# One S4D-and-PEER kernel: early query-weight pieces through half a PSUM bank, block 0 in halves, a later third inverse, and products split into rounded parts

## The chip, the cores and the metric

The kernel runs on one core of one Trainium2 chip. The time is device microseconds (us) of one execution, given as the median over several runs. Five engines of the core work side by side, each through its own list of instructions in order: PE (matmul), DVE, ACT and POOL (vector, scalar and general work), and SP, which here only issues DMA transfers. An instruction waits until the semaphores that it names have been raised by the instructions that it depends on; everything behind it on the same engine waits with it.

## What is computed

```python
x = A_u                                                   # 2048 tokens x 512
h = x + S4D(layernorm(x))                                 # K[d,l] = 2 Re sum_n C[d,n] exp(A[d,n] dt[d] l)
                                                          # y = irfft(rfft(u, 4096) * rfft(K, 4096))[:2048] + D*u
q = einsum("nd,dhc->nhc", layernorm(h), w_q)              # 32 heads, 2 x 128
i1 = argmax over e of q[..., :128] . k1[e]                # 16 experts each
i2 = argmax over e of q[..., 128:] . k2[e]
e = i1 * 16 + i2                                          # one of 256 experts per token and head
act = gelu(einsum("nd,nhd->nh", layernorm(h), u[e]))      # the softmax over one candidate is 1
out = h + einsum("nh,nhd->nd", act, v[e])
```

## The kernel before, in words

**First half, the convolution.** The 512 channels are taken in four chunks c of 128. The convolution is an FFT-like product written as matmuls in stages. For every chunk there is the spectrum of the input (`u_s1`, s1u, and `u_s2`, s2yu) and the kernel K: for each of 32 indices i (eight in a chunk) POOL makes phases and magnitudes (`pg` L552, `mg` L581 and L584), ACT takes sines (`t` L639 to L642), DVE multiplies the two into tables (`gf` L646 to L650, `mg` L654 and L659, the last one), PE sums the tables into `kps` (L685, 64 matmuls), and the result goes through s1k (L466) and s2yk (L483). The two spectra are multiplied (for c = 3 on DVE L727 and L728, ACT `ki` L734 and POOL `U` L738), and a first inverse stage `ia` (L759) gives T, of which the chunks 0 to 2 are stored in DRAM and the last stays as T3.

**The weights, beside it.** The query weights w_q are folded with the keys in 32 pieces n: `w_piece` loads 512 KB (`wq`), PE multiplies it with the key matrices ka and kb (`wps` L811, 16 records in the trace), ACT copies the result (`wt` L815), PE transposes it (`wpt` L818), ACT copies again (`wh` L822), and after every fourth piece SP stores 256 KB (`w_d` L825). When all are stored, the four quarters come back (`w_q` L897) and ACT and DVE split each into a rounded part and the rest (`w_hi` L900, `w_lo` L901). These rounded parts have the type fp32r, which PE takes at a faster rate than f32.

**Second half, PEER.** Eight blocks b of 256 tokens: `prefetch` loads Tb, cb and xt; `inverse` makes `ib` (L1005, 64 matmuls, 128 records) and adds x into h (L1012); `center` takes the mean (L1045), `hc` (L1051) and its two parts `hhi` (L1055) and `hlo` (L1059), and the square (L1072); `variance` gives `rstd`; `scores` multiplies hhi, hlo with w_hi, w_lo (`sc` L1115, for each half k of a block 24 matmuls of 512 columns) and with u (`xu` L1122, 12 matmuls of 256 columns); DVE finds the maximum (`mx` L1135, `eq`, `kq`, `ix`), and `select` transposes activations and indices (`ta`, `ixt`), broadcasts the indices (`bc`, `idxb`), builds one-hot masks on DVE (`oh` L1239), counts them on PE (`cnt` L1249), multiplies with the activations (`wt` L1257), multiplies with the expert rows v (`o` L1269, f32, 16 records a block), adds h (`ob` L1274) and stores.

**What sets the order.** One list scheduler, the class `Plan`, writes out the order of all engines' instructions beforehand. Every step is declared with an engine, an estimated cost, what it reads and writes, and which PSUM banks it takes and gives back; `BIAS` moves groups of steps (w0 to w7 are the pieces by four, tab0 to tab31 the tables, cen, inv, sc, sel the steps of a block) earlier or later in the list. `RINGS` says how many buffers a tile has. Seven PSUM banks are shared by most first-half steps (`psA`); until the parameters are done they hold parameter tiles. An eighth, `pc`, holds small statistics of the layernorm (mu_s, rs_s, dv_s) and is otherwise empty.

Of the kernel before, what the change touches and what calls it, by code (L numbers as in the profile page):

```python
# [27 lines left out]
def view(t, off, dims):  # L28
# [5 lines left out]
BIAS = dict(cen0=-321, cen1=200, cen2=494, cen3=497, cen4=149, cen5=340, cen6=-266, cen7=239, e1=358, ia0=-109,  # L34
            ia1=-262, ia2=137, ia3=-186, inv0=-5, inv1=276, inv2=455, inv3=28, inv4=-226, inv5=168, inv6=-279,
            inv7=251, k100=-188, k101=-367, k102=-393, k103=146, k110=-120, k111=-78, k112=285, k113=-195, k120=26,
            k121=138, k122=119, k123=500, k130=281, k131=65, k132=456, k133=-340, k20=1, k21=-267, k22=475, k23=455,
            par=1000, par0=-75, par1=482, pre0=-134, pre1=-400, pre2=-53, pre3=-248, pre4=22, pre5=-190, pre6=-358,
            pre7=-385, sc0=192, sc1=396, sc2=28, sc3=-3, sc4=-333, sc5=-351, sc6=208, sc7=-289, sel0=396, sel1=401,
            sel2=383, sel3=-57, sel4=143, sel5=-134, sel6=-243, sel7=-240, st=-225, tab0=-63, tab1=491, tab10=450,  # L40
            tab11=491, tab12=20, tab13=-259, tab14=96, tab15=242, tab16=320, tab17=48, tab18=-197, tab19=481,
            tab2=-105, tab20=-54, tab21=279, tab22=-344, tab23=-208, tab24=39, tab25=479, tab26=-241, tab27=-22,
            tab28=460, tab29=304, tab3=-332, tab30=-23, tab31=472, tab4=481, tab5=-171, tab6=6, tab7=-393, tab8=-37,
            tab9=-382, u100=-133, u101=99, u102=388, u103=473, u110=-377, u111=-173, u112=-171, u113=187, u120=-335,
            u121=439, u122=-81, u123=-23, u130=-213, u131=-7, u132=-347, u133=-341, u20=464, u21=-49, u22=164,
            u23=-320, var0=185, var1=-128, var2=-164, var3=178, var4=-12, var5=-16, var6=174, var7=157, w0=67,
            w1=-205, w2=320, w3=313, w4=-132, w5=344, w6=500, w7=54, wr=299)
# [3 lines left out]
class Plan:  # L51
# [5 lines left out]
    REST, SLOW = 3.0, 3.5  # L57
# [111 lines left out]
def kernel(ctx, tc, xa, xb, xt, lar, aim, cre, cim, ldt, dsk, wq, ka, kb, ue, ve,  # L169
# [39 lines left out]
    mu_s, rs_s, dv_s = pc[:, 0:64], pc[:, 64:128], pc[:, 128:256]  # L209
# [12 lines left out]
    sg, r64, w2, den, w0, dt, r = (psA.tile([P, 512], F32, tag="s", name=f"par{k}") for k in range(7))  # L222
    x_raw = [wk.tile([P, 32, 128], F32, tag="y", name=f"x{i}", bufs=2) for i in range(2)]
# [49 lines left out]
    def loads():  # L273
        def get(*p):
            for dst, src in p:
                nc.sync.dma_start(dst, src)

        for nm, dst, src in (("ld", ld_, ldt.to_broadcast([P, D])), ("lar", lar_, lar), ("aim", aim_, aim), ("cr", cr_, cre),
                             ("ci", ci_, cim)):
            plan.add("SP", 0.65, lambda dst=dst, src=src: get((dst, src)), w=[(nm, 0), (nm, 1)], lag=0.6)  # L280
        for i in range(8):
            plan.add("SP", 1.55, lambda i=i: get((x_raw[i // 4][:, 8 * (i % 4):8 * (i % 4) + 8], xa[:, 8 * i:8 * i + 8, :])),
                     w=[("x", i)], t=[f"x{i // 4}"], lag=0.6)
        plan.add("SP", 1.0, lambda: get((ca_s, ca.rearrange("p (s m) -> p s m", s=2)), (ka_s, ka), (kb_s, kb)),
                 w=["ca"], lag=0.6)
        plan.add("SP", 6.0, lambda: get((c2_s, c2.rearrange("p (k m) -> p k m", k=32))), w=["c2"], lag=0.6)

    def params():
# [76 lines left out]
        e1 = con.tile([P, 16, 256], F32, tag="T", name="e1")[:, 0:11]  # L365
# [57 lines left out]
        plan.add("SP", 0.45, lambda: nc.sync.dma_start(e_d, e1), r=["e1"], w=["e_d"], t=["e1"], lag=6.0)  # L423
# [4 lines left out]
    plan = Plan(dict(psA=7), BIAS)  # L428
# [29 lines left out]
    def stage1(dst, lhs8, kt, nm, r, tiles, key):  # L458
        for n in range(2):
# [11 lines left out]
            k = plan.add("PE", 0.93, mm, r=r, t=tiles, take="psA", n_mm=16)  # L471
            plan.add("ACT", 0.48, ev, w=[key + (kt, n)], t=tiles, give="psA", after=[k])

    def stage2(c, nm, k4, deps, tiles):
# [10 lines left out]
        return job, plan.add("PE", 0.95, mm, r=deps + ["c2"], t=tiles, take="psA", n_mm=8)  # L485


    def u_s1(c, kt):
# [16 lines left out]
        plan.add("SP", 0.45, load, w=[xs_k], t=[xs_k], lag=3.0)  # L505
# [88 lines left out]
    def factors(i, made):  # L594
# [17 lines left out]
        if i == 16:  # L612
            plan.add("SP", 0.45, e_load, r=["e_d"], w=["E1"], t=["E1"], lag=6.0)
# [55 lines left out]
    def kgen(i):  # L669
# [18 lines left out]
        plan.add("PE", 1.0, mm, r=[("tab", i, k, s) for k in range(2) for s in range(2)], w=[("kps", n)],  # L688
# [60 lines left out]
    def k_ia(c):  # L749
        plan.group = f"ia{c}"  # L750
        deps = [("P", c, k4) for k4 in range(8)]
        for n in range(8):
# [21 lines left out]
            k = plan.add("PE", 1.80, mm, r=deps + ["ca"], t=[f"yk{c}", f"yu{c}" if c > 2 else f"yk{c}", f"U{c}", f"T{c}"], take="psA", n_mm=16)  # L774
# [12 lines left out]
        if c < 3:  # L787
            for r in range(2):
                plan.add("SP", 2.0, lambda r=r: store(r), r=[("T", c, n) for n in range(8)],
                         w=[("t_d", c, r)], t=[f"T{c}"], lag=6.0)  # L790
# [3 lines left out]
    def w_piece(n):  # L794
# [4 lines left out]
        for nm, b, m in (("wq", 2, n), ("wt", 2, n), ("wh", 2, hg)):  # L799
            if m >= b:  # L800
                plan.ring(f"{nm}{m}", f"{nm}{m - b}")

        def load():
            d["in"] = tb.tile([P, 4, 2, 128], F32, tag="wq", name=f"wq{n}")
            nc.sync.dma_start(d["in"], wq[:, n])

        def mm():
            ps = bank(j1, f"wps{n}")
# [580 lines left out]
```

## Time and profile before

| quantity | value |
|---|---|
| median of 3 runs | 541.44 us (540.92 to 541.61) |
| the profiled execution, its own time | 543.62 us |
| its span in the trace | 541.8 us |
| mean granted TensorE clock | 0.974 |
| PE busy | 466.3 us of the span |

The trace holds one execution. Its rows give the start, the time busy, the engine and the line, then what is written and what is read, with the sizes. Behind some rows stands, in brackets, how long the engine was idle before and what released it; "issue" there means that no semaphore explains the wait. A row with x8 stands for eight records of the same form, and a matmul of f32 leaves two records. The time "busy" of a matmul contains its way through the array, so the pace is read from one start to the next.

### The profile page before, as it was taken

The numbers are of one execution on the slowest core, as the hardware profiler recorded it, in microseconds if no ns is written. First come the engines' busy times: TensorE is split into PE (matmuls) and PEld (weight loads), VectorE is DVE, ScalarE is ACT, GpSimd is POOL, SyncE is SP. The second block draws the span as 40 slices with busy tenths as digits, with TensorE's granted clock in tenths as the row PEclk, the third lists the DMA queues.
The fourth block names the chain that finished last, engine by engine and source line by source line (L and its number), as shares of the span: only waits on it lengthen the run. The fifth ranks groups of instructions, "written<-read, shape, count | busy, mean of one in ns | idle before, by whom it ended". The sixth has DMA issues, their size and how long they took to land. (4 is left out here: it accounts for less than half of the span.)

```text
span 541.8 us, 16659 instructions
## 1 busy us (share of the span) xinstructions
PE 466.3 (86%) x7154; PEld 397.4 (73%) x7154; DVE 410.2 (76%) x716; ACT 297.3 (55%) x588; POOL 323.0 (60%) x339
## 2 busy tenths in 40 slices
PE   0045898989999999989995975999999999999996
PEld 0024677869999899979995964878777788888765
DVE  5997857779996898699738643368796695788884
ACT  6543888984899579949973612342323333406220
POOL 0698798999989999996817004161642535066030
PEclk9999799999999999999999888999999999999997
DMA  7984586667204120300065558000402511010011
GB/s 250 404 288 137 144 247 183 194 209 270 80 2 158 41 59 3 158 1 3 2 223 179 187 185 235 0 2 1 157 1 82 182 52 40 1 40 1 2 79 40
DMA packets 27361, 61.30 MB, mean 113 GB/s; under 512 B 2932, under 2 KB 14456, under 8 KB 26136
## 3 DMA queue, kind: packets, MB, share of 16 engines
q1 hardware_dynamic: 27136, 60.11, 33.3%
q8 instruction: 56, 0.92, 0.7%
q14 instruction: 17, 0.14, 0.1%
q10 hardware_dynamic: 152, 0.13, 0.1%
HBM read 46.21 MB, written 14.02 MB: 111 GB/s over the span
## 5 line engine op out<-in xcount | busy, mean ns | idle before, releaser
L552 POOL TENSOR_TENSOR pg<-PS 128x1024 int32<-128x1024 int32 x32 | 68.6, 2148 | 5.2 <-ACT t L639 5.1
L581 POOL TENSOR_TENSOR mg<-TS 128x1024 f32<-128x1024 f32 x32 | 62.6, 1956 | 13.8 <-PE kps L685 12.6
L1150 POOL TENSOR_TENSOR ks<-kq 128x512 f32<-128x512 bf16 x16 | 18.9, 1181 | 58.6 <-DVE kq L1144 58.6
L759 PE MATMUL ia<-ca_s,U 128*128 128x128 f32 x256 | 51.4, 284 | 0.7 <-POOL U L738 0.7
L1239 DVE TENSOR_SCALAR oh<-idxb,ec_s 128x2048 bf16<-128x2048 bf16 (+1 forms) x72 | 47.6, 729 | 5.2 <-ACT idxb L1221 5.2
L1115 PE MATMUL sc<-w_hi,hhi 128*128 128x512 f32 x128 | 45.5, 437 | 0.5 <-DVE eq L1139 0.5
L811 PE MATMUL wps<-wq,ka_s 128*32 128x128 f32 x256 | 15.4, 317 | 35.1 <-DMA wq<-wq 33.3
L640 ACT ACTIVATE t<-t,halfpi 128x512 f32<-128x512 f32 x64 | 42.4, 662 | 2.1
L759 PEld LDWEIGHTS ia<-ca_s,U 128*128 128x128 f32 x256 | 40.6, 200 | 1.0 <-POOL U L738 1.0
L639 ACT ACTIVATE t<-pg 128x512 f32<-128x512 int32 x64 | 39.4, 615 | 3.4 <-DVE gf L647 2.9
L1115 PE MATMUL sc<-w_lo,hhi 128*128 128x512 f32 x128 | 40.7, 400 | 0.0
L1115 PE MATMUL sc<-w_hi,hlo 128*128 128x512 f32 x128 | 40.6, 399 | 0.0
L642 ACT ACTIVATE t<-pg 128x512 f32<-128x512 int32 x64 | 39.2, 614 | 0.8 <-DVE U L730 0.3
L759 PE MATMUL ia<-ca_s,yk 128*128 128x128 f32 x192 | 38.2, 281 | 0.0
L466 PE MATMUL s1u<-c_s,xs 128*64 128x128 f32 x512 | 34.3, 279 | 4.1 <-DVE mg L659 1.1
L584 POOL TENSOR_TENSOR mg<-TS 128x512 f32<-128x512 f32 x32 | 37.4, 1169 | 0.0
L1029 POOL TENSOR_TENSOR hs<-h 128x256 f32<-128x256 f32 x7 | 7.3, 1038 | 48.8 <-DVE h L1012 48.8
L483 PE MATMUL s2yu<-yu,c_s 128*128 128x128 f32 x256 | 32.7, 282 | 4.2 <-DVE gf L647 1.7
L685 PE MATMUL kps<-mg 128*32 128x64 f32 x1024 | 34.1, 230 | 1.9 <-issue 1.0
L811 PEld LDWEIGHTS wps<-wq,ka_s 128*32 128x32 f32 x256 | 5.9, 117 | 40.1 <-DVE pa L329 31.4
L483 PEld LDWEIGHTS s2yu<-yu,c_s 128*128 128x128 f32 x256 | 30.0, 192 | 6.3 <-ACT yk L469 1.8
L466 PEld LDWEIGHTS s1u<-c_s,xs 128*64 128x64 f32 x512 | 28.3, 138 | 8.3 <-issue 4.3
(174 smaller groups left out, 1397.0 us busy)
## 6 DMA issues: line engine op xcount, KB each, us to landing
wq<-wq SPq DMA_DIRECT2D x32, 512.0 KB, 4.3
t_d<-T SPq DMA_DIRECT2D x24, 256.0 KB, 3.7
Tb<-t_d SPq DMA_DIRECT2D x8, 768.0 KB, 5.8
x<-xa SPq DMA_DIRECT2D x8, 512.0 KB, 6.2
xs<-xb SPq DMA_DIRECT2D x16, 256.0 KB, 6.2
xt<-xt SPq DMA_DIRECT2D x8, 512.0 KB, 5.7
out<-ob SPq DMA_DIRECT2D x7, 512.0 KB, 2.7
c_s<-c SPq DMA_DIRECT2D x1, 2048.0 KB, 14.3
```

Source lines behind the costliest of these rows:

```text
L466: T.matmul(ps[64 * k:64 * k + 64, g, :], lhs8(4 * n + g), c1_s[:, k], start=True, stop=True)
L483: T.matmul(ps[:, k, :], c2_s[:, kk, :], y[:, :, kk, :], start=True, stop=True)
L552: G.tensor_tensor(view(pg, 0, [[32, 2 * NC], [8, 4], [1, 8]]), view(t["PS"], 1024 + off, [[1, 2 * NC], [128, 4], [0, 8]]), view(t["PS"], 8 ...
L581: G.tensor_tensor(view(mg, 0, [[96, NC], [8, 8], [1, 8]]), view(ts, 512 + 8 * o, [[8, NC], [1, 8], [0, 8]]), view(ts, 8 * o, [[8, NC], [0, ...
L584: G.tensor_tensor(view(mg, 64, [[96, NC], [8, 4], [1, 8]]), view(ts, 1536 + o, [[1, NC], [64, 4], [0, 8]]), view(ts, 1024 + 8 * o, [[8, NC ...
L639: A.activation(p, pg[:, :, k], AF.Abs)
L640: A.activation(p, p, AF.Sin, scale=-SINSCALE, bias=halfpi)
L642: A.activation(p, pg[:, :, k], AF.Sin, scale=SINSCALE)
L685: T.matmul(kps[32 * q:32 * q + 32, 2 * g + h, :], m[:, d, 64:96], m[:, d, 0:64], start=(e == 0), stop=(e == 1))
L759: T.matmul(ps[:, g, :], t[:, 4 * n + g].rearrange("p a b -> p (a b)"), ca_s[:, s, :], start=(s == 0), stop=(s == 1))
L1115: T.matmul(ps[:, 512 * h:512 * h + 512], t[x_][:, q, ts], I[w_][:, q, 512 * h:512 * h + 512], start=(q == 0 and x_ == w_), stop=(q == 3 an ...
L1239: V.tensor_scalar(oh[:, :, 0:ln], t["idxb"][:, :, sl], S["ec"][:, 4 * e + j:4 * e + j + 1], None, op0=ALU.is_equal)
```

## The change

It has five parts, and a sixth that follows from them.

1. **Early pieces.** The first twelve pieces (`NE = 12`) no longer take banks from `psA`. Their `wps` and `wpt` go to two 128-column parts of the bank `pc`, one of each, so one piece is in each part at a time. Pieces 2 and 3 are loaded into free parts of the parameter tile pb, piece 4 into a free part of the tile e1; ka and kb are loaded before x, and c2 behind it with an own group.
2. **Block 0 in halves.** The mean, hc, hhi, hlo and the square of block 0 are made for 128 columns at a time, and the scores of k = 0 read only the first half. Its variance comes from sums on POOL and two matmuls, as in the other blocks, in place of eight f32 matmuls.
3. **ib of block 2.** The inverses of blocks 2 and later stand behind the first quarter of block 0's scores.
4. **o of rounded products.** The product with the activations is made in place; ACT makes `whi`, DVE `wlo`, and `o` is the sum of three fp32r products (v_hi·whi, v_hi·wlo, v_lo·whi): 24 matmuls a block in place of eight f32 ones. v_hi and v_lo are made once; u and v are loaded into the buffers of w_q. whi and wlo have one buffer each.
5. **Costs in the list.** SP's steps get transfer times as costs with a shorter lag, some PE costs rise a little, REST and SLOW change.
6. `BIAS` has new numbers, so the order differs on all engines.

```diff
-    mu_s, rs_s, dv_s = pc[:, 0:64], pc[:, 64:128], pc[:, 128:256]
+    mu_s, rs_s, dv_s, wps_s, wpt_s = pc[:, 0:64], pc[:, 64:128], pc[:, 128:256], pc[:, 256:384], pc[:, 384:512]
...
-    REST, SLOW = 3.0, 3.5
+    REST, SLOW = 2.6, 6.0
...
+    NE = 12
+    plan = Plan(dict(psA=7, psW=1, psV=1), BIAS)
...
+        early = n < NE
+        home = {2: "pb", 3: "pb", 4: "e1"}.get(n, f"wq{n}")
...
+            j1["o"] = wps_s if early else bank(j1, f"wps{n}")[:, 0]
...
+            j2["o"] = wpt_s if early else bank(j2, f"wpt{n}")[:, 0]
+            T.transpose(j2["o"], d["t"], ident)
...
-        plan.add("SP", 0.45, load, w=[f"wq{n}"], t=[f"wq{n}"], lag=4.5)
-        k = plan.add("PE", 0.55, mm, r=[f"wq{n}", "ca"], t=[f"wq{n}", f"wt{n}"], take="psA", n_mm=16)
+        plan.add("SP", 1.7, load, w=[f"wq{n}"], t=[home], lag=2.6)
+        pa_, pt_ = ("psW", "psV") if early else ("psA", "psA")
+        k = plan.add("PE", 0.55, mm, r=[f"wq{n}", "ka"], t=[home, f"wt{n}"], take=pa_, n_mm=16)
...
-                             take="psD" if k is None else None, after=[] if k is None else [k], n_mm=32)
+                             take="psD" if k is None else None, after=[k] if k else [L[0]["sc"]] if b > 1 else [], n_mm=32)
...
+        if b == 0:
+            for a in range(2):
+                sl, job = slice(128 * a, 128 * a + 128), {}
...
+                k = plan.add("PE", 0.95, mm, r=["cst", ("h", b, a)], t=[kh, kc], take="psD", n_mm=8)
...
-                for q in range(4 if first else 1):
-                    lhs = t["hc"][:, q] if first else t["vs"]
-                    T.matmul(ps[:, k:k + 1], lhs[:, 128 * k:128 * k + 128], S["ones"][:, 0:1], start=(q == 0),
-                             stop=(q == 3 or not first))
+                T.matmul(ps[:, k:k + 1], t["vs"][:, 128 * k:128 * k + 128], S["ones"][:, 0:1], start=True, stop=True)
...
+            if q == 0 and k == 0:
+                t["sc"] = last
...
-                            T.matmul(ps[:, q], S["v"][:, e, 128 * (q0 + q):128 * (q0 + q) + 128], t["wt2"][:, e, sl],
-                                     start=(e == 0), stop=(e == 1))
+                            for v_, w_ in (("hi", "hi"), ("hi", "lo"), ("lo", "hi")):
+                                T.matmul(ps[:, q], S["v_" + v_][:, e, 128 * (q0 + q):128 * (q0 + q) + 128],
+                                         t["w" + w_][:, e, sl], start=(e == 0 and v_ == w_), stop=(e == 1 and v_ == "lo"))
```

**The start on PE.** Before, pieces 4 and 5 stand ahead of the first kernel sums (`kps0_0`; the number behind mg and gf is the index i).

```order
L811 MATMUL wps4_449<-wq4_397,ka_s_76 32x128 x4
L811 MATMUL wps4_449<-wq4_397,kb_s_77 32x128 x4
L818 MATMUL wpt4_465<-ident_60,wt4_459 128x128
L811 MATMUL wps5_467<-wq5_419,ka_s_76 32x128 x4
L811 MATMUL wps5_467<-wq5_419,kb_s_77 32x128 x4
L818 MATMUL wpt5_485<-ident_60,wt5_481 128x128
L685 MATMUL kps0_0_491<-mg0_366 32x64 x4
```

Now, with the pieces in `pc`:

```order
L826 MATMUL pc_96<-pb_98,ka_s_76 32x128 x4
L826 MATMUL pc_96<-pb_98,kb_s_77 32x128 x4
L834 MATMUL pc_96<-ident_60,wt2_382 128x128
L690 MATMUL kps0_0_412<-mg0_276 32x64 x4
...
L826 MATMUL pc_96<-wq5_358,kb_s_77 32x128 x4
L834 MATMUL pc_96<-ident_60,wt4_465 128x128
L826 MATMUL pc_96<-wq6_380,ka_s_76 32x128 x4
L826 MATMUL pc_96<-wq6_380,kb_s_77 32x128 x4
L690 MATMUL kps0_0_412<-mg1_352 32x64 x4
```

The sums of i = 0 moved ahead of pieces 4 and 5, and those of i = 1 stand alone behind pieces 4 to 6; each transpose here waits for a copy on ACT, and each second product for the copy of the one before it.

**The end of the convolution on PE.** Before, the last pieces are multiplied ahead of the last s2yk, and two transposes are left behind it:

```order
L811 MATMUL wps31_4129<-wq31_2888,ka_s_76 32x128 x4
L811 MATMUL wps31_4129<-wq31_2888,kb_s_77 32x128 x4
L483 MATMUL s2yk3_0_4140<-yk3_4012,c2_s_85 128x128 x4
...
L483 MATMUL s2yk3_7_4223<-yk3_4012,c2_s_85 128x128 x4
L818 MATMUL wpt30_4230<-ident_60,wt30_4138 128x128
L818 MATMUL wpt31_4234<-ident_60,wt31_4145 128x128
```

Now:

```order
L488 MATMUL s2yk3_4_4087<-yk3_3957,c2_s_85 128x128 x4
L826 MATMUL wps28_4094<-wq28_3923,ka_s_76 32x128 x4
...
L488 MATMUL s2yk3_7_4153<-yk3_3957,c2_s_85 128x128 x4
L826 MATMUL wps30_4164<-wq30_4108,ka_s_76 32x128 x4
L826 MATMUL wps30_4164<-wq30_4108,kb_s_77 32x128 x4
L834 MATMUL wpt30_4178<-ident_60,wt30_4175 128x128
L826 MATMUL wps31_4186<-wq31_4149,ka_s_76 32x128 x4
L826 MATMUL wps31_4186<-wq31_4149,kb_s_77 32x128 x4
L834 MATMUL wpt31_4216<-ident_60,wt31_4195 128x128
L764 MATMUL ia3_0_4221<-ca_s_86,yu3_2813 128x128
```

Pieces 28 to 31 moved into and behind the last s2yk, and the last stage `ia3` stands behind piece 31.

**The way into PEER on PE.** Before, with the mean of block 0 in one and the inverse of block 2 ahead of the first scores:

```order
L1045 MATMUL mean0_4535<-h0_4476,ones_d_4157 128x256 x4
...
L1005 MATMUL ib2_0_4571<-cb2_4515,Tb2_4495 32x64 x3
...
L1115 MATMUL sc0_0_4646<-w_hi_4154,hhi0_4566 128x512 x2
L1115 MATMUL sc0_0_4646<-w_lo_4155,hhi0_4566 128x512 x2
L1115 MATMUL sc0_0_4646<-w_hi_4154,hlo0_4605 128x512 x2
L1084 MATMUL var0_4660<-ones_d_4157,hc0_4559 128x1 x8
```

Now:

```order
L1086 MATMUL mean0_0_4454<-h0_4451,ones_d_4207 128x128 x4
...
L1086 MATMUL mean0_1_4499<-h0_4451,ones_d_4207 128x128 x4
...
L1143 MATMUL sc0_0_4524<-w_hi_4204,hhi0_4497 128x512 x2
...
L1029 MATMUL ib2_0_4588<-cb2_4534,Tb2_4478 32x64 x3
...
L1117 MATMUL var0_4687<-ones_d_4207,vs0_4624 128x1 x2
```

The mean stands in two halves, the first of them directly behind ib of block 0, and ib of block 2 moved behind the first scores.

221 lines of the change are left out of this document (121 added, 100 removed).

## The prediction, made before the changed kernel was run

> **What bounds the kernel now.** I first read the page's busy shares and then a table of windows cut at the borders of the stages (its columns: window, length, busy us of PE, PE's weight loads, DVE, ACT and POOL with counts, the granted TensorE clock, the share of the DMA engines, GB/s).
>
> ```profile
> PE 466.3 (86%) x7154; PEld 397.4 (73%) x7154; DVE 410.2 (76%) x716; ACT 297.3 (55%) x588; POOL 323.0 (60%) x339
> ...
> 31.40:60.00 28.60, 17.39 (x298) 11.76 (x300) 24.75 (x77) 15.21 (x37) 26.22 (x26) 1.00 0.58 175
> 60.00:280.00 220.00, 209.64 (x4102) 189.28 (x4100) 178.89 (x294) 179.00 (x354) 191.88 (x170) 0.98 0.35 113
> 280.00:296.00 16.00, 10.82 (x130) 9.92 (x126) 11.09 (x17) 7.17 (x16) 9.59 (x8) 0.98 0.55 165
> 313.40:340.00 26.60, 17.28 (x425) 14.51 (x425) 10.00 (x14) 5.42 (x7) 6.06 (x6) 0.87 0.63 190
> 340.00:525.00 185.00, 183.55 (x1915) 146.44 (x1914) 141.13 (x201) 62.51 (x102) 74.48 (x100) 1.00 0.13 44
> ```
>
> PE sets the time. It is full from 340 to 525 and close to full from 60 to 280, and idle ahead of the first piece (until 31.4), 28.6 − 17.39 = 11.2 us from there to 60, 5.2 us at the end of the convolution, 9.3 us on the way into PEER, and in the tail. A term of the sum is therefore either PE work that disappears in a full stage, or PE idle time that gets filled or shortened.
>
> **The start (parts 1 and 6).** These rows give the place.
>
> ```profile
> 36.29 0.65 PE L811 MATMUL wps<-wq,ka_s 128*32 128x128 f32 x8 [1.68 <-DMA wq<-wq]
> 36.69 0.68 PE L811 MATMUL wps<-wq,kb_s 128*32 128x128 f32 x8
> 38.64 0.65 PE L811 MATMUL wps<-wq,ka_s 128*32 128x128 f32 x8 [1.27 <-ACT wt L815]
> 40.10 0.47 PE L818 MATMUL wpt<-ident,wt 128*128 128x128 f32 x1 [0.39 <-ACT wt L815]
> 49.01 0.44 PE L685 MATMUL kps<-mg 128*32 128x64 f32 x8 [0.58 <-DVE mg L659]
> 71.13 0.32 PE L685 MATMUL kps<-mg 128*32 128x64 f32 x8
> ...
> POOL mg L581 <- PE kps L685: 11.4, 6, 2.7
> ```
>
> The first kernel sums start at 49.01, when DVE has finished the tables of i = 0 and 1 together. The list now makes table 0 first and lets its sums go ahead of pieces 4 and 5. Pieces no longer take banks that the parameters hold. I put the sums of i = 0 at about 44, 5 us earlier. POOL's magnitudes wait for these sums; six such waits between 60 and 280 add up to 11.4 us (the last row), so part of the 5 us goes on down the chain: nothing at least, 5 at most. I take 3, since the sums of i = 1 now stand behind pieces 4 to 6, whose transposes wait for ACT. The sums of i = 3, at 71.13 before, would then start near 68.
>
> What lies ahead of them differs. By the order, before that point PE had done pieces 0 to 10 and four s1u jobs; now it does pieces 0 to 11 and none of these s1u. In the full stage behind it stood 21 pieces, and now 16, since 28 to 31 moved to the last s2yk.
>
> ```profile
> 70.11 1.09 PE L466 MATMUL s1u<-c_s,xs 128*64 128x128 f32 x16
> 279.41 0.33 PE L818 MATMUL wpt<-ident,wt 128*128 128x128 f32 x1
> 279.67 1.97 PE L466 MATMUL s1k<-c_s,k 128*64 128x128 f32 x32
> 281.57 0.43 PE L811 MATMUL wps<-wq,ka_s 128*32 128x128 f32 x8
> 282.58 7.41 PE L483 MATMUL s2yk<-yk,c_s 128*128 128x128 f32 x64
> ```
>
> Two products take 282.58 − 281.57 = 1.01 us, a transpose 279.67 − 279.41 = 0.26, so a piece costs 0.76. Five fewer give 3.8; four s1u jobs of 1.09 more take 4.4. The term is 3 + 3.8 − 4.4 = **2.4 us**. Bounds: −0.6 if the sums come no earlier, and 8.4 if all 5 us arrive and about 4 of POOL's 11.4 us go too. The waits of the single bank are on PE's list as well: twelve pieces with two trips to ACT each, 24 trips. At the 0.39 of row 40.10 they come to 9.4 us, which the 11.2 idle us of this stretch hide; the third rival is about the case where they don't.
>
> **The end of the convolution (part 6).** PE stands idle here while DVE multiplies the spectra, and ia3 then runs slowly.
>
> ```profile
> 295.22 0.61 PE L759 MATMUL ia<-ca_s,yu 128*128 128x128 f32 x2 [5.02 <-DVE yu L727]
> 296.56 0.80 PE L759 MATMUL ia<-ca_s,U 128*128 128x128 f32 x2 [0.72 <-POOL U L738]
> 302.27 0.40 PE L759 MATMUL ia<-ca_s,yu 128*128 128x128 f32 x2
> 302.50 0.39 PE L759 MATMUL ia<-ca_s,U 128*128 128x128 f32 x2
> ...
> 296.00:300.00 4.00, 3.44 (x16) 3.44 (x17) 0.90 (x4) 0.04 (x1) 0.51 (x1) 0.50 0.97 377
> ```
>
> From 296.56 to 302.27 the granted clock is 0.50 and ia3 goes at about half the pace it has from 302.27 on (0.23 a row). At full pace these 5.7 us would be 2.9. Pieces 28 to 31 now fill part of the gap. From 36 to 48 PE was at 0.40 us a row of eight records, not the 0.22 to 0.24 of 281.57, though it worked almost half of the time; so a partly filled stretch need not raise the clock; here, though, PE comes into the gap at the full pace and only has to keep it. Between 0 and 2.9 I take the middle, **1.4 us**. The Trainium skill ("TensorE: Matmul & The Clock Gate", Part 1: The HAM clock gate) says that the clock goes to half after a whole idle window of about 3.4 us; by that the filled gap would keep it full and this term would be 2.9. The 5.02 idle us with the slow rows behind them agree with it; what a partly filled gap does, no run here shows.
>
> **The way into PEER (parts 2 and 3).** Now the chain from the inverse of block 0 to the first scores.
>
> ```profile
> 316.79 1.29 DVE L1012 TENSOR_TENSOR h<-ib,xt 128x512 f32<-128x512 f32 x2 [0.80 <-PE ib L1005]
> 321.76 2.47 PE L1045 MATMUL mean<-h,ones_d 128*128 128x256 f32 x8
> 324.27 1.22 DVE L1051 TENSOR_TENSOR hc<-h,mean 128x1024 f32<-128x1024 f32 x1 [1.71 <-PE mean L1045]
> 328.00 1.74 DVE L1059 TENSOR_TENSOR hlo<-hc,hhi 128x1024 fp32r<-128x1024 f32 x1
> 333.39 1.22 PE L1115 MATMUL sc<-w_hi,hhi 128*128 128x512 f32 x2
> 336.12 1.98 PE L1084 MATMUL var<-ones_d,hc 128*128 128x1 f32 x16
> ...
> PE ib L1005 <- issue: 8.2, 3, 5.0
> ```
>
> The operands of the scores are ready at 328.00 + 1.74 = 329.7, but PE is still in ib of block 2, where it stood for 5.0 us without a semaphore to wait for; the scores start at 333.39. Now: half of h at 317.4, half a mean (1.24) 318.7, half of hc 0.6, of hhi as much again (an estimate from hc, of the same size), of hlo 0.9, and handing over: about 321.2. PE meanwhile does half of ib1, the other half mean and more of ib1, some 4 us, and if the wait of about 2 us for "issue" that it has at ib1 stays, the scores start at 324.6, 8.8 us earlier. The rest of ib1 and ib2 still has to be done behind them; from 319.60 to 319.71 four records took 0.11 us at a lowered clock, and half of it is the least that a full clock can give, so these 192 records are 2.6 to 5.3 us.
>
> ```profile
> 319.60 0.34 PE L1005 MATMUL ib<-cb,Tb 128*32 128x64 f32 x3
> 319.71 0.34 PE L1005 MATMUL ib<-cb,Tb 128*32 128x64 f32 x3
> ```
>
> I take 3.3, nearer to the full clock, since these records now stand between scores: 8.8 − 3.3 = **5.5 us**. If the 5.0 us for "issue" come back behind the scores, 0.5 remain; without any such wait (2 us more, and 2.6) it is 8. The variance has two matmuls, four records, in place of 16: at 1.98 / 16 each it saves **1.5 us**, and the sums for it lie on POOL, busy 6.06 of 26.6 us here. If POOL were late, rstd would be, and xu's bank with it, not the scores.
>
> **o (part 4).** A whole block's o stands between xu and cnt.
>
> ```profile
> 510.12 0.28 PE L1122 MATMUL xu<-u_hi,hhi 128*128 128x256 f32 x1
> 511.56 3.62 PE L1269 MATMUL o<-wt,v_s 128*128 128x256 f32 x16
> 515.11 1.06 PE L1249 MATMUL cnt<-oh,hs_s 128*32 128x256 bf16 x32
> ```
>
> o takes 515.11 − 511.56 = 3.55 us. The twelve xu ahead of it, fp32r with 256 columns, the form that o gets, take 1.44, 0.12 each. 24 of them are 2.88, so a block saves 0.67, and blocks 0 to 6 save **4.7 us**, on a PE that is 183.55 of 185 us busy. By the Trainium skill ("TensorE: Matmul & The Clock Gate", Part 1) 256 columns take 256 / 2.4 GHz + 2.5 ns = 109 ns, and by that the term would be 6.5; the rows of xu are above it, so I stay with 0.12. The new DVE work (wlo, like the wt below 0.41 for half a block) is 0.7 to 0.8 us a block; DVE works 141.13 of 185 us, and ACT, which makes whi, 62.51, which hides both. Without that cover the eight blocks would cost 6 us.
>
> **The tail.**
>
> ```profile
> 517.80 1.23 DVE L1135 TENSOR_REDUCE mx<-sc 128x64 f32<-128x1024 f32 x1 [0.43 <-PE sc L1115]
> 525.89 6.42 DVE L1239 TENSOR_SCALAR oh<-idxb,ec_s 128x1024 bf16<-128x1024 bf16 x16 [0.21 <-ACT idxb L1221]
> 533.41 0.42 DVE L1257 TENSOR_TENSOR wt<-cnt,actT 128x256 f32<-128x256 f32 x1 [0.77 <-PE cnt L1249]
> 533.38 4.29 PE o L1269 x32
> ```
>
> Behind the last scores the chain is DVE's. Block 7 adds whi, wlo (0.3 + 0.8) and 48 products for o, 2.9 us at half of 0.12 and 5.8 at the pace of 256 columns, against 4.29. Ahead of its masks DVE gets block 6's wlo and its wait for cnt. That is 1 to 4 us longer. On the other side o of block 5 and half an xu, 2.88 + 1.44 us of PE, now stand behind the last scores, which come that much earlier. I set the tail to **0**, from −2 to +2.
>
> **Sum.** 2.4 + 1.4 + 5.5 + 1.5 + 4.7 + 0 = 15.5 us. The profiled execution of 543.62 us (span 541.8, 1.8 around it) would become 528.1. It lies 2.2 above the median of 541.44, so the forecast is 541.44 − 15.5 = **525.9**. All lower bounds together (−0.6, 0, 0.5, 1.5, 4.7, −2) save 4.1, which is 537.3; all upper ones (8.4, 2.9, 8, 1.5, 4.7, 2) save 27.5, which is 513.9.
>
> **Rivals.**
> *The start gives nothing and the gap closes late.* Piece 31 now stands ahead of ia3 on PE, and its load waits on SP behind a store of earlier pieces.
>
> ```profile
> wq<-wq SPq DMA_DIRECT2D x32, 512.0 KB, 4.3
> ```
>
> A load lands 4.3 us after its issue (the row's last number). If ia3 starts 3 us later and the sums no earlier, the first two terms become −0.6 and −3, and the time is 541.4 − 8.1 = 533. For it speaks that the store and the reload of w_q follow that piece too; against it that DVE, not PE, ends the gap by 5.02 us. Chance 0.22.
> *The start gives more.* POOL's 11.4 us of waits come from the same chain, PE stays at the full clock at 295, and no "issue" comes in the way: near 515. Chance 0.14.
> *Slower: the one bank at the start.* All twelve pieces go through it, and a copy on ACT stands in line with the sines. At the 1.27 us of row 38.64, 24 trips are 30.5 us, 19 more than PE has idle there; POOL then waits at every table, and with 13.1 us of other gains the end would be near 548. It decides from (11.2 + 13.1) / 24 = 1.0 us a trip. Most trips before (0.39) are far below. Chance 0.06.
> *The change does not do what it says:* the terms spend themselves in waits that this trace can't show, and the time stays within 0.2%: 0.04.
>
> **Numbers.** The forecast has 0.54, with its own range of 519 to 531. Faster by over 0.2% (about what a measurement of this kernel can tell from none) is 0.54 + 0.22 + 0.14 = 0.90, within it 0.04, slower 0.06. The range from 513 to 536 leaves out the slow rival, no change and a little of both ends.
>
> **What would show it.** Right: the first sums near 44 and those of i = 3 near 68; a start of ia3 no later behind the last s2yk's begin than 14 us (282.58 to 296.56); the first scores 9 us nearer to ib0; o at about 2.9 us a block. Wrong: waits of PE for `wt` or `wh` of 1 us and more in a row in the first 70 us; an ia3 that waits for a piece; an "issue" of 5 us that only moves behind the first scores; DVE above 90% in the blocks.

## The result, and the profile after

The changed kernel takes 546.83 us (median of 10 runs, 542.55 to 551.14); the kernel before, measured beside it, 541.21 (10 runs, 534.49 to 544.0). The ratio is 1.0105, its 95% interval 1.0059 to 1.0151. A second set of 12 runs gave 544.74 against 541.93 and 1.0057 (1.0008 to 1.0105). So the change is slower by 0.6 to 1%; 525.9 and faster had been forecast. (The ratios leave out disturbed runs, so they can differ a little from the quotient of the medians.)

The page of the changed kernel gives the busy time of each engine as before, and its windows are cut at its own stages (columns as in the prediction).

```profile
PE 466.2 (86%) x7222; PEld 398.9 (74%) x7222; DVE 424.7 (79%) x728; ACT 300.5 (56%) x598; POOL 327.6 (61%) x342
```

```profile
28.80:60.00 31.20, 17.97 (x306) 12.20 (x308) 26.33 (x79) 15.82 (x39) 29.59 (x30) 0.90 0.56 191
60.00:280.00 220.00, 205.63 (x4004) 187.00 (x4002) 180.82 (x297) 175.45 (x343) 189.88 (x170) 0.98 0.31 98
280.00:297.30 17.30, 15.36 (x220) 13.43 (x215) 10.59 (x16) 10.23 (x24) 9.11 (x8) 1.00 0.60 199
311.00:340.00 29.00, 23.53 (x467) 19.85 (x466) 18.37 (x26) 9.30 (x15) 7.49 (x9) 0.94 0.80 250
340.00:525.00 185.00, 179.46 (x2069) 142.99 (x2071) 157.15 (x227) 65.52 (x113) 77.56 (x100) 0.99 0.14 50
525.00:540.80 15.80, 11.25 (x68) 10.61 (x57) 2.56 (x5) 0.81 (x2) 0.00 (x0) 0.50 0.13 34
```

PE has as much to do as before (466.2 against 466.3 us). Between 60 and 280 it is busy 4.0 us less than before (205.63 against 209.64 of the same 220 us); between 340 and 525, mostly blocks, it is idle 5.5 of 185 us where it was 1.5; and the last 15.8 us run at a granted clock of 0.50. The chain of waits shows what the end of the tail consists of (start, length, engine, line):

```profile
522.16 2.47 DVE oh L1269 x6
...
524.67 0.84 PE cnt L1279 x29
...
525.96 0.34 DVE wlo L1294
...
526.34 10.30 PE o L1309 x47
...
536.67 0.69 DVE ob L1314
```

The o of block 7 alone takes 10.30 us on the path that sets the end; before it was 4.29.

To see where the time went I cut both executions at four marks: the start of the last s2yk, the first scores, the end of the last scores, and the end. Each kernel was profiled a second time later (last two columns).

| stretch | forecast | before | after | difference | before, again | after, again | difference |
|---|---|---|---|---|---|---|---|
| start to last s2yk | −2.4 | 282.58 | 284.41 | +1.8 | 281.6 | 282.1 | +0.5 |
| to first scores | −10.2 | 50.8 | 39.65 | −11.2 | 47.3 | 39.9 | −7.4 |
| to end of last scores | −7.2 | 184.3 | 183.0 | −1.3 | 187.7 | 182.1 | −5.6 |
| to the end | +4.3 | 24.1 | 33.8 | +9.7 | 24.5 | 33.8 | +9.3 |
| span | −15.5 | 541.8 | 540.8 | −1.0 | 541.1 | 537.9 | −3.2 |

The forecast column is the sum of the prediction, regrouped: 1.4 + 8.8 for the way to the first scores; in the blocks 4.7 + 1.5, less 3.3 for the displaced ib, and 4.3 for the o of block 5 and the half xu that move behind the last scores, which then stand against it in the tail.

The spans are 1.0 and 3.2 us shorter, the medians 5.6 and 2.8 us longer. That is the choice of executions: those of the change were among its shorter ones (4.3 and 5.1 us below the medians), those of the kernel before lay above the medians that these are set against (by 2.4 and 1.0 us). So the traces show where the gain of 15.5 us is missing, but not what makes the other executions of the change longer than the profiled ones. One number is there for every execution, the mean granted clock: its median is 0.972 over 29 runs of the kernel before and 0.963 and 0.964 over the 10 and 12 of the change.

### The profile page after: what moved, and what is told of

The parts are those of the page before. It is cut to its first block, busy times and chain, and to the rows that moved or that the text cites. A ratio compares the mean times of both kernels' runs of the same rounds, so it can differ in the third digit from the quotient of the medians.

```text
span 540.8 us, 16831 instructions
## 1 busy us (share of the span) xinstructions
PE 466.2 (86%) x7222; PEld 398.9 (74%) x7222; DVE 424.7 (79%) x728; ACT 300.5 (56%) x598; POOL 327.6 (61%) x342
## 5 line engine op out<-in xcount | busy, mean ns | idle before, releaser
L1269 DVE TENSOR_SCALAR oh<-idxb,ec_s 128x2048 bf16<-128x2048 bf16 (+1 forms) x72 | 51.1, 776 | 1.0 <-ACT idxb L1251 0.9
L764 PE MATMUL ia<-ca_s,U 128*128 128x128 f32 x256 | 49.6, 275 | 0.7 <-POOL U L743 0.7
L764 PEld LDWEIGHTS ia<-ca_s,U 128*128 128x128 f32 x256 | 38.9, 192 | 0.9 <-POOL U L743 0.9
L826 PE MATMUL pc<-wq,ka_s 128*32 128x128 f32 x72 | 5.0, 361 | 36.8 <-DMA wq<-wq 28.8
L488 PE MATMUL s2yu<-yu,c_s 128*128 128x128 f32 x256 | 31.3, 279 | 3.3 <-DVE U L735 1.6
L488 PEld LDWEIGHTS s2yu<-yu,c_s 128*128 128x128 f32 x256 | 29.6, 192 | 4.8 <-PE s2yu L488 1.9
L471 PE MATMUL s1k<-c_s,k 128*64 128x128 f32 x512 | 32.6, 284 | 0.5 <-ACT U L525 0.5
L690 PE MATMUL kps<-gf 128*32 128x64 f32 x1024 | 32.8, 225 | 0.0
```

The lines of the kernel that those rows point to most:

```text
L471: T.matmul(ps[64 * k:64 * k + 64, g, :], lhs8(4 * n + g), c1_s[:, k], start=True, stop=True)
L488: T.matmul(ps[:, k, :], c2_s[:, kk, :], y[:, :, kk, :], start=True, stop=True)
L690: T.matmul(kps[32 * q:32 * q + 32, 2 * g + h, :], m[:, d, 64:96], m[:, d, 0:64], start=(e == 0), stop=(e == 1))
L764: T.matmul(ps[:, g, :], t[:, 4 * n + g].rearrange("p a b -> p (a b)"), ca_s[:, s, :], start=(s == 0), stop=(s == 1))
L1269: V.tensor_scalar(oh[:, :, 0:ln], t["idxb"][:, :, sl], S["ec"][:, 4 * e + j:4 * e + j + 1], None, op0=ALU.is_equal)
```

## The experiments

**The change again (e4), unchanged.** It gives the second pair of columns above, and the base for the others of its set.

> The changed kernel once more, as the comparison for the others and for a second profile. Its profile so far is at the fast end of its times (542.55 of 542.55 to 551.14). If the tail alone makes it slow, a second profile has the same stage lengths up to the last scores (507 us). If the early stage varies, one with a longer time loses its microseconds ahead of 324 us, the start of the first scores.

Measured 544.74 us (538.4 to 548.53, 12 runs). The tail of 33.8 us came back to the tenth; the stretches ahead of it differ by up to 3.5 us between two executions of one kernel.

**Block 7's o once, 256 columns wide (e1).** One set of 24 products behind both halves of the masks, in place of two sets of 24 with 128 columns.

```diff
+            if b == 7 and lo == 0:
+                p0 = p
+                continue
+            if b == 7:
+                sl, ln, c_ = slice(0, 256), 256, 1.0
```

> The changed kernel, with o of block 7 made once for all 256 columns behind both halves (24 products of 256 columns in place of 48 of 128). Width theory (a rounded product of 128 columns takes as long as one of 256, so the split doubles o): o of block 7 takes half of the 10.3 us, about 5.2 us at the half clock, and the kernel is about 5 us faster than the changed one. Clock theory (only the half clock of the tail makes o slow, and the products cost by their columns): 24 x 256 columns take the same 10.3 us, no gain.

**Block 7's o in f32, as before the change (e2).** No whi and wlo there; the products of the two halves stay.

```diff
+                            if b == 7:
+                                T.matmul(ps[:, q], S["v"][:, e, 128 * (q0 + q):128 * (q0 + q) + 128], t["actT"][:, e, sl],
+                                         start=(e == 0), stop=(e == 1))
+                                continue
```

> The changed kernel, with o of block 7 in f32 as before (32 records of 128 columns, no whi and wlo there). Width theory: f32 records of 128 columns cost 0.107 us at full and 0.213 at half clock, so o takes 4.3 us as before to 6.8 at half clock, without the 0.8 us for whi and wlo: 4 to 7 us faster than the changed one. Clock theory: the same, since 32 records are fewer than 48. It tells how much of the tail is the split, whatever the cause.

e1 took 538.98 us (533.94 to 544.27), e2 537.75 (535.62 to 541.21), 12 runs each: 5.8 and 7.0 less than the change in the same set. From the chains of waits of the two, e1 first, the piece that answers to the 10.30:

```profile
529.01 5.52 PE o L1314 x24
```

```profile
524.63 5.70 PE o L1311 x32
```

So the o of e1 takes what the width theory had for it (5.2), not 10.3. Behind the last scores e1 has 29.4 us and e2 26.3, in place of 33.8. Since e2 leaves more of PE's work in the blocks, blocks and tail together are the fairer number: 212.9 and 211.1 us, against 216.8 and 215.9 in the two traces of the change and 208.4 and 212.2 in those of the kernel before. The spans (538.9 and 534.5) hold the spread of the first half as well. The mean clock has a median of 0.974 in both sets of runs, about what it was before the change. The edit of e2 was repeated on two other variants below and gave −4.1 (e5 to e6) and −3.6 us (e10 to e11). Against the kernel before, e1 stands at 1.0031 (0.998 to 1.0083) and e2 at 1.0017 (0.9975 to 1.0059): the medians are lower, but the intervals hold 1, so neither is shown to beat it.

**What a rounded product costs by width (e3, e12).** In block 3, where the clock is full, o was split by columns: two halves of 128 (48 products, e3), or four quarters of 64 (96 products, e12).

```diff
-                        for e in range(2):
+                        for z, e in [(z, e) for z in (((0, 128), (128, 128)) if b == 3 else ((0, ln),)) for e in range(2)]:
```

> The changed kernel, with o of block 3, in the middle of the full stage at the full clock, split into 48 products of 128 columns. Width theory: 48 x 0.107 to 0.12 = 5.1 to 5.8 us for o of block 3 against 2.8, and the end 2.3 to 3 us later. Clock theory: 48 x 0.06 = 2.9 us, and no change.

> The changed kernel, with o of block 3 in 96 products of 64 columns, at the full clock. The 128 columns took 0.112 us each and the 256 columns 0.118. If a narrow rounded product takes four passes like f32, 64 columns cost half of 0.112, 0.056 each, and o 5.4 us as with 128. If a product cannot be shorter than its weight load, 0.11 each whatever the width, and o 10.7 us, 5 us more on the end.

From the timeline of PE in e3, two rows of its 128-column products, the second 42 products behind the first:

```profile
440.34 0.28 PE L1309 MATMUL o<-wlo,v_hi 128*128 128x128 f32 x1
...
445.03 0.27 PE L1309 MATMUL o<-wlo,v_hi 128*128 128x128 f32 x1
```

(445.03 − 440.34) / 42 = 0.112 us each, against 0.118 for 256 columns: half the columns cost almost the same. From the timeline of e12, 64-column products (the first stands at 441.31) and others 5 us later, then the clock of these stretches from its windows:

```profile
443.91 0.28 PE L1309 MATMUL o<-whi,v_hi 128*128 128x64 f32 x1
444.02 0.28 PE L1309 MATMUL o<-wlo,v_hi 128*128 128x64 f32 x1
...
449.27 0.40 PE L1309 MATMUL o<-whi,v_hi 128*128 128x64 f32 x1
449.49 0.40 PE L1309 MATMUL o<-wlo,v_hi 128*128 128x64 f32 x1
```

```profile
440.00:444.00 4.00, 4.00 (x37) 4.00 (x37) 3.59 (x6) 0.47 (x1) 3.69 (x7) 1.00 0.73 206
448.00:452.00 4.00, 4.00 (x20) 4.00 (x21) 0.27 (x1) 0.00 (x0) 0.00 (x0) 0.50 0.00 0
```

A quarter of the columns costs 0.11 us too, so the price goes by the number of products. PE's weight loads are busy all of the time (the second busy column), which fits a bound by the loading of weights; that this is the bound was not tried by itself. And PE, busy for 4.00 of 4.00 us, went from clock 1.00 to 0.50 in the middle of these narrow products: o of block 3 took 16.3 us (441.31 to 457.59) in place of 2.8, where 5.4 or 10.7 had been expected. The single run of e12, 559.02 us, is longer than every run of the change; that of e3, 547.43, lies among them (538.4 to 551.14).

**The statistics out of the bank (e5, e6).** mu, rstd and the difference of the layernorm move from `pc`, which the early pieces use, to a tile in SBUF. e6 is e5 with the o of e2.

```diff
-    mu_s, rs_s, dv_s, wps_s, wpt_s = pc[:, 0:64], pc[:, 64:128], pc[:, 128:256], pc[:, 256:384], pc[:, 384:512]
+    stat = con.tile([P, 256], F32, name="stat")
+    mu_s, rs_s, dv_s, wps_s, wpt_s = stat[:, 0:64], stat[:, 64:128], stat[:, 128:256], pc[:, 256:384], pc[:, 384:512]
```

> The changed kernel, with the layernorm statistics (mu_s, rs_s, dv_s) in a tile of their own in SBUF, so that the bank pc holds the early pieces alone. Bank theory (DVE's statistics and subtractions wait for pieces only because they share pc; that eats the lead of the first sums): DVE's waits for pieces between 59 and 83 us (about 9.9 us) go, the lead of about 5.5 us at the sums of i = 0 is still 3 us or more at i = 4 (77 instead of 79.5), and the last s2yk starts 3 to 5 us earlier (near 280). Chain theory (the middle is paced by ACT, POOL and PE in turn, whatever the start): the waits go, but from i = 12 on the sums stand where they stood, and the last s2yk within 1 us of 284.

> Both repairs in the changed kernel: statistics in SBUF, and o of block 7 in f32. If the two add: the 7 us of the f32 o of block 7 and 3 to 5 of the bank theory, a median near 533 to 535. By the chain theory near 537.5, as with the first repair alone.

e5 took 561.88 us (ratio 1.0416, 1.0354 to 1.0478), e6 557.79 (1.0319, 1.0257 to 1.0381). DVE's waits for pieces did go, 9.9 us between 55 and 90 in the change and none here. But the sums of i = 4 start at 78.47 (e5) and 77.17 (e6), against 79.48 and 78.06 in the two traces of the change: about 1 us for them. Even that is not clear of the spread, since e1, e2, e3, e8 and e12, whose start is that of the change, have them between 78.26 and 81.13. And the edit had a price of its own. First the group of subtractions on DVE (columns: busy us, mean ns of one, idle before) in the change, then in e5:

```profile
L505 DVE TENSOR_TENSOR xs<-xs,pc 128x512 f32<-128x512 f32 x16 | 10.8, 683 | 6.0 <-ACT wh L838 2.2 <-DMA xs<-xb 1.9 <-PE pc L834 1.1
```

```profile
L506 DVE TENSOR_TENSOR xs<-xs,stat 128x512 f32<-128x512 f32 x16 | 25.0, 1583 | 1.9 <-DMA xs<-xb 1.9
```

The same subtraction costs 1.58 us in place of 0.68 once its second operand lies in SBUF. The product behind it goes from 10.7 to 22.6 us, together 26.1 us more on DVE. So the total of e5 says nothing about the bank; the mark at i = 4, where 77 had been expected if the bank were the cause, is what can be used of it.

**Fewer early pieces (e10, e11).** Eight in place of twelve go through the bank; e11 has the o of e2 as well.

```diff
-    NE = 12
+    NE = 8
```

> The changed kernel, with eight early pieces through pc in place of twelve (NE = 8); pieces 8 to 11 take banks of psA, as before, so no piece is in pc any more once the statistics are written there. Bank theory: DVE's waits for pieces between 59 and 83 us (9.9 us together) shrink to 3 or less, the sums of i = 4 start near 76 instead of 79.5, and the last s2yk starts 2 to 4 us earlier than the changed kernel's 284; median 2 to 4 us lower. Chain theory: the waits shrink, but the last s2yk stays within 1 us of 284 and the median near 545.

> Eight early pieces and o of block 7 in f32. Bank theory: 2 to 4 us under the 537.75 of the f32 o of block 7 alone, 534 to 536. Chain theory: 537 to 539.

568.06 us (1.0546, 1.0418 to 1.0674) and 564.46 (1.044, 1.0311 to 1.057). DVE's longest wait for a piece, 3.9 us, is still there in e10, and the sums of i = 4 start at 78.43 and 78.01, where 76 had been expected. The sums of i = 31 start at 273.70 and 272.21, 2.7 and 4.2 us earlier than in the change, but the list came out otherwise and the last s2yk begins at 295.6 and 294.1, some 10 us later. The total therefore tells nothing of the bank. What the bank costs over the whole first half stays open; at i = 4 it is about 1 us, within the spread.

**The splits of w_q earlier in the list (e7).** `wr` is the group of the steps that bring w_q back; in the change T3's copies on DVE stand behind its `w_lo`.

```diff
-w7=94, wr=489, xl=495)
+w7=94, wr=0, xl=495)
```

> The changed kernel, with the number of the group wr (load and split of w_q) from 489 to 0, which puts all w_hi and w_lo behind the copies of T3 on ACT and DVE, and the loads of w_q behind those of Tb and cb. Copy theory (ib of block 0 starts 2 to 4 us behind ia3's end because T3's copies stand between the splits): ib0 starts within 0.5 us of ia3's end. What then counts is whether the first scores keep this: if the splits are late, the scores wait for w_hi and nothing is won (324 or later); if not, they start near 321. Load theory (ib0 waits for cb or xt): ib0 waits as before.

568.57 us (1.0531, 1.0466 to 1.0597). Rows of PE's timeline, then of ACT's:

```profile
316.33 0.26 PE L1029 MATMUL ib<-cb,Tb 128*32 128x64 f32 x3 [1.01 <-ACT wh L838]
...
332.37 2.08 PE L1086 MATMUL mean<-h,ones_d 128*128 128x128 f32 x8 [13.56 <-DVE h L1036]
```

```profile
324.03 1.04 ACT L917 CAST w_hi<-w_q 128x1024 fp32r<-128x1024 f32 x1 [7.76 <-DMA w_q<-w_d]
```

The wait ahead of ib is 1.01 us in place of 3.95, with T3's copies no longer behind the splits. But a split waits 7.76 us for the transfer that brings w_q back, h stands behind the splits on DVE, and the mean waits 13.56 us for it: the first scores begin at 339.7, some 15 us later than in the change. What was taken off one engine's queue came out behind a transfer.

**Every o in f32 (e8).** No whi or wlo at all.

```diff
+                            if True:
+                                T.matmul(ps[:, q], S["v"][:, e, 128 * (q0 + q):128 * (q0 + q) + 128], t["actT"][:, e, sl],
+                                         start=(e == 0), stop=(e == 1))
+                                continue
```

> The changed kernel with every o in f32 as before, no whi, wlo at all (the rounded v is still made). Against the changed kernel with only block 7 in f32 (median 537.75): if the rounded products are worth their 0.7 us a block, 4.7 us more, near 542.5. If DVE is what holds PE in the blocks, the 5 us of wlo that fall away give some of it back and the loss is 1 to 3 us.

547.33 us (545.7 to 548.73, 6 runs; ratio 1.0132, 1.0082 to 1.0183), 9.6 more than e2, which differs from it in blocks 0 to 6 alone, and more than either expectation. The rounded products there gain, then, though not all of the 9.6 is theirs, since the order of the list changed with them. The first scores begin at 325.12 and the last end at 520.44.

**The kernel before, once more (e13).** Its trace gives the fifth and sixth numbers of the rows in the table.

> The kernel before once more, for a second profile: its times spread from 533 to 545, and its first profile (543.62) is at the slow end. If the spread comes from PE's clock at the start, a faster one gains its microseconds ahead of 120 us; if from the way into PEER, between 295 and 340 us; if from the tail, behind 525.

542.88 us in one run. Its tail is 24.5 us (24.1 at first).

## Why the prediction was wrong

**The tail is the step that failed, with the start and the blocks beside it.** Of the three it is the one that the experiments settle. The prediction put "48 products for o, 2.9 us at half of 0.12 and 5.8 at the pace of 256 columns", and set the tail to 0 because work moves out from under the last scores. The mechanism it named is there: PE's work of 4.3 us did move behind the last scores. What it had wrong is the time of o. Rows of PE's timeline in the changed kernel and a window inside this stretch:

```profile
526.62 0.41 PE L1309 MATMUL o<-whi,v_lo 128*128 128x128 f32 x1
526.83 0.41 PE L1309 MATMUL o<-whi,v_hi 128*128 128x128 f32 x1
```

```profile
529.00:533.00 4.00, 4.00 (x20) 4.00 (x20) 0.69 (x1) 0.00 (x0) 0.00 (x0) 0.50 0.00 0
```

One product starts every 0.213 us: 47 of them make the 10.30. Two things are in this. Half the width brought nothing: at the full clock e3 has 0.112 us for 128 columns, so 48 products are 5.4 us, near the upper of the prediction's two values. The other 5 us are the clock, which the prediction had not put into this term at all: it was 0.50 for the whole of o. In the kernel before, the 32 f32 records of the same o came in at 0.50 too, but had the full clock again after 0.9 us:

```profile
533.38:534.30 0.92, 0.92 (x4) 0.92 (x5) 0.42 (x1) 0.00 (x0) 0.00 (x0) 0.50 0.00 0
534.40:537.67 3.27, 3.25 (x29) 3.06 (x28) 0.69 (x1) 0.00 (x0) 0.00 (x0) 1.00 0.03 9
```

Over the whole tail the mean clock is 0.76 in both traces of the change, against 0.85 and 0.86 in the kernel before and 0.86 and 0.87 in e1 and e2. Of the 9.7 us that the tail grew, 6.9 are o (525.49 to 536.65, with 0.85 of waiting for wlo, against 4.29), 1.5 lie between the last scores and the masks of block 7, where the moved work and block 6's wlo stand, and 1.2 between the masks and o, where DVE now adds block 6's h between the two halves of the masks (1.28 us). e1 and e2 take 4.4 and 7.5 us off the stretch and 5.8 and 7.0 off the median.

PE was busy without a gap from 529 to 533 and the clock stayed at 0.50; it did so for all 10.3 us. The Trainium skill ("TensorE: Matmul & The Clock Gate", Part 1: The HAM clock gate) has the full clock come after one busy window of about 3.4 us of sustained work. By that, as an estimate, the last 7 us of o would have run at 0.112 and ended some 3 us earlier. The trace does not agree for rounded products of 128 columns here. With 256 columns (e1) the full clock came back about 5 us after the first product (0.21 us a product from 529.85 on, 0.12 from 534.12 on), and with the f32 records of 128 columns in e2 about 4 us after the first (0.50 until 528.6, 1.00 from there on).

**The start.** Forecast −2.4, measured +1.8 and +0.5. The last s2yk begins between 282.1 and 285.5 in the seven traces whose start is that of the change (the change, e1 to e4, e8, e12), and at 282.6 and 281.6 in those of the kernel before, so there is no gain here. PE's sums of the tables:

```profile
43.47 0.44 PE L690 MATMUL kps<-mg 128*32 128x64 f32 x8 [3.93 <-DVE mg L664]
...
69.51 0.44 PE L690 MATMUL kps<-mg 128*32 128x64 f32 x8
...
79.48 0.32 PE L690 MATMUL kps<-mg 128*32 128x64 f32 x8
```

The first sums are at 43.47, 5.5 us earlier, as forecast (44). Those of i = 3 are 1.6 us earlier (2.4 in the second pair), where 3 had been taken. Then comes the loss: i = 4 is 3.5 us later than before (76.01). The groups of PE between i = 3 and i = 4, before and after:

```profile
L466 PE MATMUL s1u<-c_s,xs 128*64 128x128 f32 x34 | 2.5, 279 | 0.0
```

```profile
L471 PE MATMUL s1u<-c_s,xs 128*64 128x128 f32 x96 | 6.9, 315 | 0.0
```

The additional records are the four s1u jobs of the prediction, 4.4 us, and one s1k; they run at a clock of 0.76 (0.85 in the second trace; before it was 1.00 from 70 to 80), and PE stood waiting ahead of them (busy 5.80 of 10 us from 60 to 70, at a clock of 0.84; before 9.18, at 0.66). The window from i = 3 to i = 4 in the changed kernel:

```profile
69.51:79.48 9.97, 9.97 (x184) 9.33 (x174) 6.47 (x11) 8.13 (x15) 9.15 (x9) 0.76 0.40 112
```

Against these 4.4 us, 3.8 were to come back from five pieces fewer. The stretch from i = 4 to the last s2yk is only 1.6 us shorter (206.57 to 204.93): three of the pieces fall into it, PE's work falls by 2.5 us and its idle time grows by 0.8. A stage in which PE is 95% busy did not give back the whole of the work that it lost.

The "slower" rival, the one bank, is not what did it up to i = 4: DVE waits 3.9 us in one piece for a copy of it and 9.9 in all there, but without these waits (e5, e6) i = 4 comes at most about 1 us earlier. That the prediction had not separated: waits that are long in the list of one engine need not be on the path.

**The gap and ia3.** Forecast −1.4. From the start of the last s2yk to the last row of ia3 the first pair has 30.6 and 27.9 us, −2.7; the second has 29.4 and 29.6, nothing. Rows of the first trace of the change:

```profile
296.06 0.43 PE L826 MATMUL wps<-wq,ka_s 128*32 128x128 f32 x8 [0.95 <-DMA wq<-wq]
...
298.39 0.49 PE L764 MATMUL ia<-ca_s,U 128*128 128x128 f32 x2 [0.69 <-POOL U L743]
298.72 0.39 PE L764 MATMUL ia<-ca_s,yu 128*128 128x128 f32 x2
298.94 0.39 PE L764 MATMUL ia<-ca_s,U 128*128 128x128 f32 x2
...
312.34 0.39 PE L764 MATMUL ia<-ca_s,U 128*128 128x128 f32 x2
```

PE has no idle piece above 0.95 us in the gap, and ia3 goes at 0.22 us a row from its first rows on: the full clock, and the upper end of 0 to 2.9. The second trace of the change has the same order, no idle piece above 1.31 us, and still lost the clock in ia3:

```profile
296.00:300.00 4.00, 3.90 (x20) 3.90 (x21) 0.68 (x5) 0.76 (x3) 0.04 (x1) 0.58 0.65 180
```

The rule of the Trainium skill that the prediction weighed here ("TensorE: Matmul & The Clock Gate", Part 1: The HAM clock gate), the half clock after a whole idle window of about 3.4 us, agrees with the first trace and not with the second. Of the seven traces with this gap, ia3 has a clock of 1.00 in three (the first trace of the change, e2, e8) and of 0.86 to 0.90 in four (e1, e3, e4, e12), so the −2.7 was luck, and the prediction's doubt about a partly filled stretch was right. Piece 31 did wait for its load, 0.95 us (1.31 in the second trace), short of the 3 us of the first rival.

**The way into PEER.** From the last row of ia3 to the first scores 20.2 us became 11.7, 8.5 less, and 17.9 became 10.4, 7.6 less, in the second pair, against a forecast of 8.8.

```profile
316.67 0.33 PE L1029 MATMUL ib<-cb,Tb 128*32 128x64 f32 x3 [3.95 <-DMA sel_f<-sel]
...
324.06 0.73 PE L1143 MATMUL sc<-w_hi,hhi 128*128 128x512 f32 x2
```

A new wait of 3.95 us stands ahead of ib; the row names a transfer, but on DVE T3's last copies, which ib reads, stand behind the splits:

```profile
313.58 1.23 DVE L918 TENSOR_TENSOR w_lo<-w_q,w_hi 128x1024 fp32r<-128x1024 f32 x1
314.72 1.74 DVE L777 COPY T<-ia 64x256 f32<-64x256 f32 x4
```

They end at 316.46, just ahead of ib's 316.67 (313.98 and 314.19 in the second trace), and e7 shortens the wait to 1.01 us by the order of the splits alone. The scores were then 7.4 us behind ib, where it had been 19.9: the halves gave more than was forecast, and the copies took it.

**The blocks.** Windows from the first scores to the end of the last, before and after:

```profile
333.39:517.69 184.30, 182.85 (x1873) 146.19 (x1873) 136.63 (x194) 61.45 (x99) 71.73 (x96) 0.99 0.15 50
```

```profile
324.06:507.03 182.97, 178.34 (x2038) 141.24 (x2033) 150.71 (x203) 64.84 (x107) 79.83 (x101) 0.99 0.19 64
```

PE's work fell by 4.5 us and its idle time grew from 1.45 to 4.63. The sizes of the work were right: o of a block 2.82 us (2.88 forecast),

```profile
507.03 0.28 PE L1309 MATMUL o<-whi,v_hi 128*128 128x256 f32 x1
...
509.85 0.28 PE L1150 MATMUL xu<-u_hi,hhi 128*128 128x256 f32 x1
```

with 24 products to the next xu; the first variance 0.50 us in place of 1.98; the displaced ib 2.96 us of PE in 324 to 340 (3.3 forecast). What came on top are waits of PE, 1.5 us each for "issue" at ib and for DVE's masks:

```profile
PE ib L1029 <- issue: 1.5, 1, 1.5
PE cnt L1279 <- DVE oh L1269: 1.5, 3, 0.9
```

That DVE would hide wlo was too easy: DVE's busy time rose by 14 us in this stretch (136.63 to 150.71), to 82%, and cnt waits for it three times. In all PE waits 1.7 us for DVE here in each trace of the change, and 0.8 in each of the kernel before. The second pair has −5.6 in this stretch, since that trace of the kernel before has a longer one (187.7, with 2.6 us of "issue" at ib). The mark at the first scores moves between the two traces of the kernel before: the stretch ahead of it goes from 50.8 to 47.3, the one behind it from 184.3 to 187.7. So the way into PEER and the blocks are better taken together: 235.1 and 235.0 us before, 222.6 and 222.0 after, 12.5 and 13.0 less, where 17.4 had been forecast. Which of their terms are short by these 4 to 5 us was not tried; PE's idle time in the blocks, which grew by 3.2 us in the first pair and 2.5 in the second, is the larger part.

**In sum,** the two pairs of traces miss 14.5 and 12.3 us of the gain: 4.2 and 2.9 at the start, 4.9 and 4.4 between the last s2yk and the end of the last scores, and 5.4 and 5.0 in the tail. The tail is the only one that an experiment gave back, and by that the change is level with the kernel before (e2, 1.0017), not faster; start and blocks are located, with causes that are in part argued. Open stays why the median of the change lies 4 to 5 us above its two profiled executions. In the first pair the lower mean clock (0.966 in place of 0.974) has a place: a tail of 33.8 us at 0.76 in place of 24.1 at 0.85 loses 4.5 us of full clock, which is 0.008 of the span. The medians of the change are lower still (0.963 and 0.964) and back at 0.974 in e1 and e2; where the longer executions lose more, no trace tells.

## What to carry to other kernels

A split into rounded products trades one long product for three short ones, and below 256 columns (128 and 64 were tried) it costs by the number of products, not by their width: use it where the tiles are wide, and keep the plain product in a last, halved tile that nothing hides. Work that leaves an engine with 95% of its time busy can come back in part as idle time (0.8 of 2.5 us here), so price a removal in such a stage by the stretch between two marks and not by the sum of its rows. A single profiled execution can lie several us from the median; where a stage is to be judged, profile both kernels twice and see which differences stay.

## What the runs showed of the hardware that was not expected

- A rounded (fp32r) product, with a weight load for each, took 0.118 us with 256 columns, 0.112 with 128 and 0.112 with 64 at the full clock; at 0.50 it took 0.213 with all three.
- A busy PE does not hold or win the full clock with narrow rounded products: with 64 columns it fell from 1.00 to 0.50 about 4.5 us after the first of them (441.31; e12), with 128 columns at 0.50 it stayed there for 10.3 us. 128 columns that came in at the full clock kept it for 5 us in block 3 of e3, and lost it 1.6 us after the first of them in the tail of e12 (543.10 to 544.7). f32 records of 128 columns won it back (kernel before, e2).
- A gap that is filled for the most part (PE busy 10.9 to 11.5 of 12.7 to 14.1 us, no idle piece above 1.5) was followed by a clock of 1.00 in three traces and by one of 0.86 to 0.90, with pieces at 0.50, in four, with PE's work in the same order.
- An element-wise operation of DVE on two f32 operands in SBUF (the subtraction and the product of e5, L506 and L509) took 0.69 us while POOL stood idle and 2.63 beside a POOL operation, which itself took 2.59 us there and 2.15 elsewhere. Rows of e5, DVE and then POOL (idle from 86.8 to 92.7):

```profile
80.77 2.63 DVE L506 TENSOR_TENSOR xs<-xs,stat 128x512 f32<-128x512 f32 x1
...
87.37 0.69 DVE L509 TENSOR_TENSOR xs<-xs,stat 128x512 f32<-128x512 f32 x1
```

```profile
80.26 2.59 POOL L558 TENSOR_TENSOR pg<-PS 128x1024 int32<-128x1024 int32 x1
...
85.17 1.61 POOL L590 TENSOR_TENSOR mg<-TS 128x512 f32<-128x512 f32 x1
92.65 2.14 POOL L558 TENSOR_TENSOR pg<-PS 128x1024 int32<-128x1024 int32 x1 [5.87 <-ACT t L645]
```
